# Value products on all 128 weight columns: heads and rests side by side in local and global attention

## The chip, the cores and the metric

The kernel runs on one core of one Trainium2 chip. The metric is the device time of one execution in microseconds (us), the median of several runs. The engines named are PE (TensorE; PEld is its weight load), DVE (VectorE), ACT (ScalarE), POOL (GpSimd) and SP (SyncE, whose queue issues the transfers here).

## The reference

Attention with local and global tokens, followed by a two-layer product with a squared ReLU:

```python
batch, n_heads, seq_l, seq_g, head_dim = (8, 8, 512, 32, 64)
window, scale = 32, 1 / sqrt(64)
# global queries see all 544 keys
out_g = sm(scale * q_g @ k_all.T) @ v_all
# local queries see the 32 global keys and the local ones at a distance of at most 32
s_ll = where(abs(pos[:, None] - pos[None, :]) <= window, scale * q_l @ k_l.T, -1e9)
out_l = sm(concat([scale * q_l @ k_g.T, s_ll])) @ concat([v_g, v_l])
x = concat([out_g, out_l]) as 8 * 544 rows of 8 * 64 = 512
h = maximum(x @ w_in, 0)          # w_in 512 x 2048
out = (h * h) @ w_out             # w_out 2048 x 512
```

All is float32. `sm` is a softmax over the last axis.

## The kernel before

**Two-part numbers.** Most products run in the type float32r, which holds fewer bits than float32. A value a is therefore split into a head a_h (the rounded copy, made on ACT) and a rest a_l = a - a_h (a subtraction on DVE), and a product a b is summed as a_h b_h + a_l b_h + a_h b_l. Only the first 16 heads ("plain") use plain float32.

**Steps.** A unit of attention is one head of one half sequence, 256 queries (t = 0 to 127; 16 units make one batch). One step t of the main loop interleaves: the second half of the attention of unit t - 1 (transposes of its probabilities, value product, evacuation), the first half of unit t (scores, softmax), the splitting of the inputs of unit t + 1, and one slice of the two-layer product, m = t - 9: `gemm1(m)` makes a slice h of 256 hidden columns for 256 rows (24 matmuls), `act1` and `act2` make its squared ReLU and split it into `gh` and `gl`, and `gemm2(m - 1)` adds the slice of before to the output sums (12 matmuls). The last steps have no attention.

**Order.** From t = 17 on (`FREE`) every instruction of PE, DVE and ACT keeps the order of the program text on its engine (class `InOrder`). Engines meet only in semaphores on data. So the order below is that of the queues. In step t with attention:

- `transposes(t-1)`, `scores(t)` and `gemm1(m, 0)` on PE
- `pt_split(t-1)`: ACT copies the transposed probabilities out of the PSUM tile `pt` as heads
- `softmax1(t)`: DVE adds the mask and takes the maximum of each half (`prob <- s`), and scales it
- `softmax2(t)`: ACT takes two Exp with sums
- `pt_rest(t-1)`: DVE subtracts the heads from `pt`
- jobs of the global attention (place 3), then `evac` of a finished output block
- `gemm1(m, 1)`, `av(t-1)` (the value product, into the PSUM tile `xa`), `g_scores(t)` on PE
- `softmax3(t)`: DVE makes the reciprocal, and the two halves of `prob` are scaled
- `act1(m)`: Relu on ACT, and the square on ACT or on DVE (`SQ` lists the residues of t modulo 16 with ACT)
- `x_evac(t-1)`: ACT copies the head `x_h` out of `xa`, DVE makes the rest `x_l`
- `split_head(t+1)`: ACT copies the heads `hi` of the next unit's keys, queries and values, DVE makes the rests
- `g_evac`, `g_load`, jobs (place 2), `gemm2(m-1, 0)`, `gemm2(m-1, 1)`, `act2(m)` (`gh` on ACT, `gl` on DVE), jobs (place 1)

The global attention of four heads at a time (32 queries each) is done in jobs over eight steps, twice in 16 steps: `g_soft`, `g_exp`, `g_norm`, `g_tr` (transposes into a tile of the PSUM buffer `xa`), `g_rest`, `g_split_v`, `g_av` (the value product for a pair of heads, into the same PSUM buffer `xa`, of which there is one) and `g_x`. In a period of 16, `g_av` falls in steps 1, 4, 7 and 14, `g_tr` in 3 and 13, `g_split_v` in 0, 4, 6 and 14, `g_x` in 2, 5, 8 and 15, `g_soft` in 2 and 12, `evac` in 2 and 10; `g_evac` in every odd step.

**Value product before.** For one unit: weights of 64 columns (a block of values), 128 moving columns (queries). Two blocks of keys take three products each, a middle block of 64 keys, doubled over the 128 rows, takes two, and the 32 global keys, stacked over the rows as head, head and rest, take one of 256 moving columns. That is nine matmuls into one [64, 256] result. A pair of global heads: four blocks of keys with three products and one last block, 13 matmuls of 64 weight columns and 128 moving ones.

All instructions of PE, DVE and ACT are recorded under line 52, in the helper `InOrder`; they are told apart by their tiles.

Of the kernel before, what the change touches and what calls it, by code (L numbers as in the profile page):

```python
# [7 lines left out]
F32 = mybir.dt.float32  # L8
F32R = mybir.dt.float32r
I32 = mybir.dt.int32  # L10
AF = mybir.ActivationFunctionType
# [5 lines left out]
P = 128  # L17
HALF = 256
NGR = 2 * B
NT = NGR * H  # L20
# [9 lines left out]
PLAN = [",,,b", "b,,,b", "b,,,b", "b,,b,", "b,,b,", "b,,b,", "b,,b,", "b,b,,b", "b,b,,b", "bb,bb,bb,bb", "bb,bb,bb,bb", "bbs,bb,bbs,bbs", "bbs,bbs,bbs,bbs", "bbs,bbs,bbs,bbs", "bbs,bbs,bs,s", "ss,s,s,s", "ss,s,s,s", "s,,s,", "s,,s,", "s,,s,", "s,,s,", "s,,s,", "s,,s,"]  # L30
FREE = (17, 17, 17)
LOOK = 2
SQ = (2, 3, 4, 5, 14, 15)
MUL = 9
WCH = 32

# [1 line left out]
def f(ap):  # L38
    return ap.bitcast(F32)
# [19 lines left out]
def attention_moe(  # L59
# [22 lines left out]
    def plain(t):  # L82
        return t < NPLAIN
# [41 lines left out]
    def split_head(t):  # L125

        hd = heads[t]
        raw = hd["raw"]
        if plain(t):
            return  # L130
        hi = p2.tile([P, PK], F32R, tag="hi", name=f"hi{t}")
        lo = p2.tile([P, QC + 192], F32R, tag="lo", name=f"lo{t}")
        ac.copy(hi, raw)
        ve.tensor_sub(lo, raw[:, KC : KC + QC + 192], f(hi[:, KC : KC + QC + 192]))
        ve.tensor_sub(hi[64:, :KC], raw[64:, :KC], f(hi[64:, :KC]))
        ve.tensor_sub(hi[32:64, PK - 64 :], raw[32:64, PK - 64 :], f(hi[32:64, PK - 64 :]))
        hd["hi"], hd["lo"] = hi, lo

    def scores(t):
# [45 lines left out]
    def softmax3(t):  # L185
        st = heads[t]["st"]
        pr = prob[t % 2]
        ve.tensor_scalar(out=st[:, 6:8], in0=st[:, 4:6], scalar1=1e-9, scalar2=None, op0=ALU.add)
        ve.reciprocal(out=st[:, 0:2], in_=st[:, 6:8])
        for u in range(2):  # L190
            w_ = pr[:, WIN * u : WIN * (u + 1)]
            if MUL <= t < NPLAIN:
                ac.activation(out=w_, in_=w_, func=AF.Copy, scale=st[:, u : u + 1])
            else:
                ve.tensor_scalar(out=w_, in0=w_, scalar1=st[:, u : u + 1], scalar2=None, op0=ALU.mult)
# [6 lines left out]
    def pt_split(t):  # L202
        hd = heads[t]
        if plain(t):
            pts = p2.tile([P, 512], F32, tag="gh", name=f"pts{t}")
            ac.copy(pts, pt)
            hd["pts"] = pts
            return
        ph = p1.tile([P, 640], F32R, tag="ph", name=f"ph{t}")
        pl = p1.tile([P, 256], F32R, tag="pl", name=f"pl{t}")  # L210
        ac.copy(ph[:, :256], pt[:, :256])
        ac.copy(ph[:64, 256:384], pt[:64, 320:448])
        for r in (0, 32):
            ac.copy(ph[r : r + 32, 384:640], pt[64:96, 256:512])
        hd["ph"], hd["pl"] = ph, pl

    def pt_rest(t):
        if plain(t):
            return
        ph, pl = heads[t]["ph"], heads[t]["pl"]  # L220
        ve.tensor_sub(pl, pt[:, :256], f(ph[:, :256]))
        ve.tensor_sub(ph[64:, 256:384], pt[:64, 320:448], f(ph[:64, 256:384]))

        ve.tensor_sub(ph[64:, 384:640], pt[64:, 256:512], f(ph[:64, 384:640]))

    def av(t):
        hd = heads[t]
        c = QC + KC
        if plain(t):

            xa = ps_a.tile([P, HALF], F32, tag="xa", name=f"xa{t}")
            v, pts = hd["raw"][:, c:], hd["pts"]
            mm = [
                (xa, v[:, 0:128], pts[:, 256:512]),
                (xa[:, 0:128], v[:, 64:192], pts[:, 0:128]),
                (xa[:, 128:256], v[:, 128:256], pts[:, 128:256]),
            ]
        else:
            xa = ps_a.tile([64, HALF], F32, tag="xa", name=f"xa{t}")
            vh, vl, ph, pl = hd["hi"][:, c:], hd["lo"][:, QC:], hd["ph"], hd["pl"]  # L240
            mm = []
            for u in range(2):
                o, vs, ps = xa[:, 128 * u : 128 * u + 128], slice(64 * u, 64 * u + 64), slice(128 * u, 128 * u + 128)
                mm += [(o, vh[:, vs], ph[:, ps]), (o, vl[:, vs], ph[:, ps]), (o, vh[:, vs], pl[:, ps])]
            o = xa[:, 64:192]
            mm += [(o, vh[:, 128:192], ph[:, 256:384]), (o, vl[:, 128:192], ph[:, 256:384])]
            mm.append((xa, vh[:, 192:256], ph[:, 384:640]))
        for i, (o, a, b) in enumerate(mm):
            pe.matmul(o, a, b, start=i == 0, stop=i == len(mm) - 1, skip_group_check=True)
        hd["xa"] = xa[:64, :]  # L250

    def x_evac(t):
        g, h = divmod(t, 8)
        xa = heads[t]["xa"]
        r = slice((h % 2) * 64, (h % 2) * 64 + 64)
        if g == 0:
            ac.copy(xg[r, h // 2, :], xa)
        else:
            ac.copy(x_h[r, g % 2, h // 2, :], xa)
            ve.tensor_sub(x_l[r, g % 2, h // 2, :], xa, f(x_h[r, g % 2, h // 2, :]))  # L260
        heads[t] = None

    state = {}
# [1 line left out]
    def g_load(t):  # L265

        b, grp = t // 16, (t // 4) % 2

        def cols(z, j):
            return bass.AP(z.tensor, z.offset + 64 * j, [list(z.ap[0]), [256, 2], [160, 2], [1, 32]])  # L270

        src = qg[b, grp].rearrange("p (a b) n -> p a b n", a=2)
        if plain(t):
            qz = p1.tile([P, 512], F32, tag=("ph", "gvl", "gvh", "ph")[t // 4], name=f"qz{t}")
            nc.gpsimd.memset(qz, 0.0)
            qr = p1.tile([P, 2, 2, 32], F32, tag="qr", name=f"qr{t}")
            (nc.sync if t else nc.scalar).dma_start(qr, src)
            nc.gpsimd.tensor_copy(cols(qz, 0), qr)
        else:
            qz = qgz  # L280
            qr = p1.tile([P, 2, 2, 32], F32, tag="qr", name=f"qr{t}")
            nc.sync.dma_start(qr, src)
            ac.copy(cols(qgz, 0), qr)
            ve.tensor_sub(cols(qgz, 1), qr, f(cols(qgz, 0)))
        state["qz"] = qz
# [32 lines left out]
    def g_split_v(t, pair):  # L318

        gv = state["gv"]  # L320
        gvh = p1.tile([P, 5, P], F32R, tag="gvh", name=f"gvh{t}_{pair}")
        gvl = p1.tile([P, 4, P], F32R, tag="gvl", name=f"gvl{t}_{pair}")
        ac.copy(gvh, gv)
        ve.tensor_sub(gvl, gv[:, :4, :], f(gvh[:, :4, :]))
        ve.tensor_sub(gvh[32:64, 4, :], gv[32:64, 4, :], f(gvh[32:64, 4, :]))
        state["gvs"] = gvh, gvl

    def g_soft(t):
        s = sg[:, (t // 4) % 2, :]
# [17 lines left out]
    def g_tr(t):  # L347

        s = sg[:, (t // 4) % 2, :]
        gt = ps_a.tile([P, 512], F32, tag="xa", name=f"gt{t}")  # L350
        for c in range(4):
            pe.transpose(gt[:, 128 * c : 128 * c + 128], s[:, 128 * c : 128 * c + 128], ident)
        pth = p1.tile([P, 640], F32R, tag="pth", name=f"pth{t}")
        ac.copy(pth[:, :512], gt)
        state["gpt"] = pth, gt

    def g_tr_last(t):

# [4 lines left out]
        state["ge"] = ge  # L363

    def g_rest(t):
        (pth, gt), ge = state["gpt"], state["ge"]
        ptl = p1.tile([P, 512], F32R, tag="ptl", name=f"ptl{t}")
        ac.copy(pth[:64, 512:], ge[:64, :])
        ve.tensor_sub(ptl, gt, f(pth[:, :512]))
        ve.tensor_sub(pth[64:, 512:], ge[64:, :], f(pth[:64, 512:]))  # L370
        state["gpt"] = pth, ptl

    def g_av(t, pair):
        (gvh, gvl), (pth, ptl) = state["gvs"], state["gpt"]
        xo = ps_a.tile([64, P], F32, tag="xa", name=f"gxo{t}_{pair}")
        mm = []
        for c in range(4):
            cols = slice(128 * c + 64 * pair, 128 * c + 64 * pair + 64)
            mm += [(pth[:, cols], gvh[:, c, :]), (pth[:, cols], gvl[:, c, :]), (ptl[:, cols], gvh[:, c, :])]
        mm.append((pth[:, 512 + 64 * pair : 576 + 64 * pair], gvh[:, 4, :]))  # L380
        for i, (x, y) in enumerate(mm):
            pe.matmul(xo, x, y, start=i == 0, stop=i == len(mm) - 1)
        xs = p1.tile([64, P], F32, tag="xs", name=f"gxs{t}_{pair}")
        ac.activation(out=xs, in_=xo, func=AF.Copy, scale=state["gst", t][:64, pair : pair + 1])
        state["xs"] = xs

    def g_x(t, pair):
# [71 lines left out]
    def act1(m):  # L459
        hp = moe["hp"]  # L460
        pool, tag = (p2, "gl") if m < 8 else (p1, "r")
        r = pool.tile([P, 2, HALF], F32, tag=tag, name=f"r{m}")
        ac.activation(out=r, in_=hp, func=AF.Relu)
        if m < 8 or m + LAG < NT + 8 and (m + LAG) % 16 in SQ:
            ac.activation(out=r, in_=r, func=AF.Square)
        else:
            ve.tensor_mul(r, hp, r)
        moe["r"] = r
# [33 lines left out]

    def evac(blk, tiles=(0, 1)):
        for i in tiles:
            pool, tag = ((p1, "ot"), (p2, "gl"))[i]
            ot = pool.tile([P, DM], F32, tag=tag, name=f"ot{blk}_{i}")
            ac.copy(ot, moe["o"][i])
            if blk < NGR:
# [262 lines left out]
```

## Time and profile before

| | |
|---|---|
| median of 3 runs | 1068.76 us (1068.66 to 1069.08) |
| profiled execution | 1068.82 us, span 1067.0 us |
| granted PE clock | 1.000 of full speed |
| PE busy | 1050.4 us, 98% |
| PE weight loads | 941.7 us, 88% |
| DVE busy | 856.3 us, 80% |
| ACT busy | 753.1 us, 71% |
| 16 steps in the steady part | 122.28 us |

How rows are read. A row of the timeline has the start in us from the span's start, the duration, the engine, the line, the operation, the tiles (out <- in), their shapes and how many instructions are merged (x2), and in brackets the idle time before it with what ended it. A row of groups has the busy time in us and the mean of one in ns, then the idle time before the group. A row of windows has the stretch, its length, the busy time of PE, PEld, DVE, ACT and POOL with instruction counts, the granted clock, the share of the transfer engines and GB/s. A row of waits has who waited for whom, the total, the number of times and the longest.

### The profile page before, as it was taken

What the parts mean: (1) busy time and instruction counts of PE and PEld (TensorE: products, weight loads), DVE (VectorE), ACT (ScalarE), POOL (GpSimd) and SP (SyncE); (2) the same over time, 40 slices, a digit from 0 to 9 for tenths busy, and PEclk for the clock granted to TensorE, in tenths of its full rate; (3) what the DMA queues carried; (4) which work ended last, traced back from release to release, by engine and by line L of the source; (5) the groups of instructions that cost most, each with busy time, mean ns of one, the idle gap of its engine ahead of it and who ended that gap; (6) DMA issues with size and microseconds to landing.
All of it is one profiled execution on the core that took longest, in us unless ns stands there. A gap on an engine that the chain in (4) does not pass through costs nothing.

```text
span 1067.0 us, 21142 instructions
## 1 busy us (share of the span) xinstructions
PE 1050.4 (98%) x7568; PEld 941.7 (88%) x7568; DVE 856.3 (80%) x2687; ACT 753.1 (71%) x1901; POOL 3.9 (0%) x14
## 2 busy tenths in 40 slices
PE   7999999999999999999999999999999999999998
PEld 6776889999998989998999989999999989999896
DVE  5698988898888989988888888888888888874321
ACT  5898877778777776778777777777777787774322
POOL 1000000000000000000000000000000000000000
PEclk9999999999999999999999999999999999999999
DMA  9772132223222322222322222223221322201000
GB/s 372 310 263 74 57 106 76 71 80 98 68 89 64 103 65 83 74 91 77 94 71 82 86 72 76 90 66 100 78 89 55 94 86 66 88 29 33 13 20 20
DMA packets 54312, 96.78 MB, mean 91 GB/s; under 512 B 4288, under 2 KB 29376, under 8 KB 54208
## 3 DMA queue, kind: packets, MB, share of 16 engines
q1 hardware_dynamic: 54064, 95.37, 27.2%
q8 instruction: 60, 0.98, 0.4%
q14 instruction: 44, 0.36, 0.1%
q10 hardware_dynamic: 144, 0.07, 0.0%
HBM read 86.51 MB, written 8.91 MB: 89 GB/s over the span
## 4 chain that ended last, share of the span: by engine, by line
PE 87%; ACT 7%; DVE 4%; issue 1%; DMA 0%; ACTq 0%
PE o L52 33%; PE h L52 32%; PE xa L52 7%; PE s L52 6%; PE pt L52 5%; PE gxo L52 2%; PE gs L52 2%; ACT prob L52 1%; DVE prob L52 1%; ACT r L52 1%; ACT ph L52 1%; ACT hi L52 1%; ACT ot L52 1%; PE gt L52 1%; ACT sg L52 0%
## 5 line engine op out<-in xcount | busy, mean ns | idle before, releaser
L52 PE MATMUL h<-x_h,ws 128*128 128x256 f32 x2048 | 388.9, 283 | 0.0
L52 PEld LDWEIGHTS h<-x_h,ws 128*128 128x128 f32 x2048 | 327.0, 191 | 0.5
L52 PE MATMUL o<-ws,gh 128*128 128x512 f32 x1024 | 321.3, 395 | 0.0
L52 PE MATMUL h<-x_l,ws 128*128 128x256 f32 x1024 | 289.1, 282 | 0.1
L52 PEld LDWEIGHTS o<-ws,gh 128*128 128x128 f32 x1024 | 185.5, 188 | 34.6
L52 PE MATMUL o<-ws,gl 128*128 128x512 f32 x512 | 202.6, 396 | 0.0
L52 PEld LDWEIGHTS h<-x_l,ws 128*128 128x128 f32 x1024 | 195.9, 191 | 0.9 <-DVE x_l L52 0.4
L52 ACT CAST ph<-pt 128x256 fp32r<-128x256 f32 x448 | 141.1, 341 | 67.7 <-PE pt L52 60.8
L52 ACT ACTIVATE prob<-prob,st 128x224 f32<-128x224 f32 x270 | 127.8, 475 | 61.2 <-DVE st L52 59.1
L52 ACT ACTIVATE r<-h 128x512 f32<-128x512 f32 x136 | 81.4, 599 | 112.3 <-PE h L52 112.3
L52 PEld LDWEIGHTS o<-ws,gl 128*128 128x128 f32 x512 | 96.2, 188 | 22.7
L52 DVE CUSTOM_DVE_ANT_0 prob<-s,con 128x224 f32<-128x224 f32 x256 | 90.0, 386 | 24.5 <-PE s L52 23.2
L52 DVE TENSOR_TENSOR gl<-r,gh 128x512 fp32r<-128x512 f32 x128 | 87.9, 686 | 23.3 <-ACT gh L52 20.5
L52 ACT CAST hi<-raw 128x864 fp32r<-128x864 f32 x112 | 102.5, 915 | 1.4
L52 DVE TENSOR_TENSOR r<-h,r 128x512 f32<-128x512 f32 x82 | 56.7, 692 | 51.9 <-ACT r L52 50.6
L52 PE MATMUL xa<-ph,hi 128*64 128x128 f32 x448 | 87.3, 238 | 1.6 <-DVE ph L52 1.2
L52 DVE TENSOR_TENSOR hi<-raw,hi 64x352 fp32r<-64x352 f32 x224 | 82.5, 368 | 6.4
L52 ACT CAST gh<-r 128x512 fp32r<-128x512 f32 x128 | 79.1, 618 | 9.1 <-DVE r L52 8.7
L52 DVE TENSOR_TENSOR ph<-pt,ph 64x128 fp32r<-64x128 f32 x224 | 79.6, 355 | 7.0
L52 DVE TENSOR_TENSOR lo<-raw,hi 128x448 fp32r<-128x448 f32 x112 | 69.6, 622 | 15.3 <-ACT hi L52 12.5
L52 PE MATMUL pt<-con,prob 128*128 128x128 f32 (+1 forms) x512 | 78.2, 274 | 0.7 <-ACT prob L52 0.5
L52 DVE TENSOR_SCALAR prob<-prob,st 128x224 f32<-128x224 f32 x242 | 70.7, 334 | 4.1
(80 smaller groups left out, 1572.7 us busy)
## 6 DMA issues: line engine op xcount, KB each, us to landing
raw<-in_pk_dram SPq DMA_DIRECT2D x127, 432.0 KB, 3.2
wr<-in_w_dram SPq DMA_DIRECT2D x32, 512.0 KB, 7.9
gv<-in_vg_dram SPq DMA_DIRECT2D x32, 320.0 KB, 3.3
out_dram<-ot SPq DMA_DIRECT2D x32, 256.0 KB, 2.2
qr<-in_qg_dram SPq DMA_DIRECT2D x31, 64.0 KB, 2.8
out_dram<-ot SPq DMA_DIRECT2D x8, 64.0 KB, 1.7
con<-in_consts_dram SPq DMA_DIRECT2D x2, 224.0 KB, 5.1
raw<-in_pk_dram SPq DMA_DIRECT2D x1, 304.0 KB, 3.2
```

The lines of the kernel that those rows point to most:

```text
L52: r = method(*args, **kwargs)
```

## The change

The weights of a value product become 128 columns wide: a block of values stands as 64 columns of heads with 64 columns of rests beside it. The probabilities' heads and rests stand side by side too, as 256 moving columns. One matmul then makes all four products of the parts (also rest by rest): in the rows 0 to 63 of its result stand the products with the values' heads, in the rows 64 to 127 those with the values' rests, and in two column groups those with the probabilities' heads and rests.

- `split_head`: `hi` holds keys and queries, four value blocks of head and rest (64 + 64 columns each), and the queries' rests `lo`. ACT makes two copies instead of one; DVE makes the rests of the values in an operation of its own.
- `pt_split`, `pt_rest`: one tile `ps` in place of `ph` and `pl`; the two 32-row copies of the global keys become one of 64 rows.
- `av`: four matmuls, one of 128 and three of 256 moving columns, into a whole PSUM bank. The first two write columns in two runs.
- `x_evac`: the parts are added on DVE: `xr` = heads' product - `x_h`, then + the second column group, then + the rows 64 to 127.
- `g_split_v`, `g_tr`, `g_rest`: the same parts, laid side by side in one tile.
- `g_av`: five matmuls, four of 256 moving columns and one of 64 weight columns and 128 moving ones; then a copy on ACT, two adds on DVE, and the scaling on ACT.
- `softmax3`: for units from 16 on the second half is scaled on ACT, not DVE.
- `act1`: for all steps with attention the square is made on ACT; `SQ` goes.
- `evac`: the output tile `ot` of the first half shares the buffer of `pth`; a tile of the start takes the buffer `r`; the host packs the global values twice, not three times.

```diff
-SQ = (2, 3, 4, 5, 14, 15)
...
-        hi = p2.tile([P, PK], F32R, tag="hi", name=f"hi{t}")
-        lo = p2.tile([P, QC + 192], F32R, tag="lo", name=f"lo{t}")
-        ac.copy(hi, raw)
-        ve.tensor_sub(lo, raw[:, KC : KC + QC + 192], f(hi[:, KC : KC + QC + 192]))
+        c = QC + KC
+        hi = p2.tile([P, c + 2 * VC + QC], F32R, tag="hi", name=f"hi{t}")
+        lo = hi[:, c + 2 * VC :]
+        vr = raw[:, c:].rearrange("p (b n) -> p b n", b=4)
+        vs = hi[:, c : c + 2 * VC].rearrange("p (b n) -> p b n", b=4)
+        ac.copy(hi[:, :c], raw[:, :c])
+        ac.copy(vs[:, :, :64], vr)
+        ve.tensor_sub(lo, raw[:, KC:c], f(hi[:, KC:c]))
...
-        ve.tensor_sub(hi[32:64, PK - 64 :], raw[32:64, PK - 64 :], f(hi[32:64, PK - 64 :]))
+        ve.tensor_sub(vs[:, :, 64:], vr, f(vs[:, :, :64]))
...
-            if MUL <= t < NPLAIN:
+            if MUL <= t < NPLAIN or t >= NPLAIN and u == 1:
...
-        ph = p1.tile([P, 640], F32R, tag="ph", name=f"ph{t}")
-        pl = p1.tile([P, 256], F32R, tag="pl", name=f"pl{t}")
-        ac.copy(ph[:, :256], pt[:, :256])
-        ac.copy(ph[:64, 256:384], pt[:64, 320:448])
-        for r in (0, 32):
-            ac.copy(ph[r : r + 32, 384:640], pt[64:96, 256:512])
-        hd["ph"], hd["pl"] = ph, pl
+        ps = p1.tile([P, 896], F32R, tag="ph", name=f"ph{t}")
+        pb = ps[:, :512].rearrange("p (u h n) -> p u h n", u=2, h=2)
+        ac.copy(pb[:, :, 0, :], pt[:, :256].rearrange("p (u n) -> p u n", u=2))
+        ac.copy(ps[:64, 512:640], pt[:64, 320:448])
+        ac.copy(ps[:64, 640:], pt[64:, 256:])
+        hd["ps"], hd["pb"] = ps, pb
...
     def pt_rest(t):
...
-        ph, pl = heads[t]["ph"], heads[t]["pl"]
-        ve.tensor_sub(pl, pt[:, :256], f(ph[:, :256]))
-        ve.tensor_sub(ph[64:, 256:384], pt[:64, 320:448], f(ph[:64, 256:384]))
-        ve.tensor_sub(ph[64:, 384:640], pt[64:, 256:512], f(ph[:64, 384:640]))
+        ps, pb = heads[t]["ps"], heads[t]["pb"]
+        ve.tensor_sub(pb[:, :, 1, :], pt[:, :256].rearrange("p (u n) -> p u n", u=2), f(pb[:, :, 0, :]))
+        ve.tensor_sub(ps[64:, 512:640], pt[:64, 320:448], f(ps[:64, 512:640]))
+        ve.tensor_sub(ps[64:, 640:], pt[64:, 256:], f(ps[:64, 640:]))
...
     def av(t):
...
-            xa = ps_a.tile([64, HALF], F32, tag="xa", name=f"xa{t}")
-            vh, vl, ph, pl = hd["hi"][:, c:], hd["lo"][:, QC:], hd["ph"], hd["pl"]
-            mm = []
-            for u in range(2):
-                o, vs, ps = xa[:, 128 * u : 128 * u + 128], slice(64 * u, 64 * u + 64), slice(128 * u, 128 * u + 128)
-                mm += [(o, vh[:, vs], ph[:, ps]), (o, vl[:, vs], ph[:, ps]), (o, vh[:, vs], pl[:, ps])]
-            o = xa[:, 64:192]
-            mm += [(o, vh[:, 128:192], ph[:, 256:384]), (o, vl[:, 128:192], ph[:, 256:384])]
-            mm.append((xa, vh[:, 192:256], ph[:, 384:640]))
+            xa = ps_a.tile([P, 512], F32, tag="xa", name=f"xa{t}")
+            xb = xa.rearrange("p (u h n) -> p u h n", u=2, h=2)
+            ps, vs = hd["ps"], [hd["hi"][:, c + 128 * i : c + 128 * i + 128] for i in range(4)]
+            both = bass.AP(xa.tensor, xa.offset + 64, [list(xa.ap[0]), [192, 2], [1, 64]])
+            mm = [(both, vs[2], ps[:, 512:640]), (xb[:, :, 0, :], vs[3], ps[:, 640:])]
+            mm += [(xa[:, 256 * u : 256 * u + 256], vs[u], ps[:, 256 * u : 256 * u + 256]) for u in range(2)]
...
-        hd["xa"] = xa[:64, :]
+        hd["xa"] = xa
...
     def x_evac(t):
...
-            ac.copy(xg[r, h // 2, :], xa)
+            ac.copy(xg[r, h // 2, :], xa[:64, :])
+            heads[t] = None
+            return
+        x0, x1 = x_h[r, g % 2, h // 2, :], x_l[r, g % 2, h // 2, :]
+        if plain(t):
+            ac.copy(x0, xa[:64, :])
+            ve.tensor_sub(x1, xa[:64, :], f(x0))
...
-            ac.copy(x_h[r, g % 2, h // 2, :], xa)
-            ve.tensor_sub(x_l[r, g % 2, h // 2, :], xa, f(x_h[r, g % 2, h // 2, :]))
+            xb = xa.rearrange("p (u h n) -> p u h n", u=2, h=2)
+            x0, x1 = [x.rearrange("p (u n) -> p u n", u=2) for x in (x0, x1)]
+            xr = p1.tile([P, 2, P], F32, tag="xr", name=f"xr{t}")[r]
+            ac.copy(x0, xb[:64, :, 0, :])
+            ve.tensor_sub(xr, xb[:64, :, 0, :], f(x0))
+            ve.tensor_add(xr, xb[:64, :, 1, :], xr)
+            ve.tensor_add(x1, xb[64:, :, 0, :], xr)
...
-            qz = p1.tile([P, 512], F32, tag=("ph", "gvl", "gvh", "ph")[t // 4], name=f"qz{t}")
+            qz = p1.tile([P, 512], F32, tag=("ph", "r", "gvh", "ph")[t // 4], name=f"qz{t}")
...
     def g_split_v(t, pair):
...
-        gvh = p1.tile([P, 5, P], F32R, tag="gvh", name=f"gvh{t}_{pair}")
-        gvl = p1.tile([P, 4, P], F32R, tag="gvl", name=f"gvl{t}_{pair}")
+        gvs = p1.tile([P, 9, P], F32R, tag="gvh", name=f"gvh{t}_{pair}")
+        gvh, gvl = gvs[:, :5, :], gvs[:, 5:, :]
...
-        state["gvs"] = gvh, gvl
+        state["gvs"] = gvs
...
-        pth = p1.tile([P, 640], F32R, tag="pth", name=f"pth{t}")
-        ac.copy(pth[:, :512], gt)
-        state["gpt"] = pth, gt
+        pts = p1.tile([P, 1152], F32R, tag="pth", name=f"pth{t}")
+        pc = pts[:, :1024].rearrange("p (c h n) -> p c h n", c=8, h=2)
+        gc = gt.rearrange("p (c n) -> p c n", c=8)
+        ac.copy(pc[:, :, 0, :], gc)
+        state["gpt"] = pts, pc, gc
...
     def g_rest(t):
-        (pth, gt), ge = state["gpt"], state["ge"]
-        ptl = p1.tile([P, 512], F32R, tag="ptl", name=f"ptl{t}")
-        ac.copy(pth[:64, 512:], ge[:64, :])
-        ve.tensor_sub(ptl, gt, f(pth[:, :512]))
-        ve.tensor_sub(pth[64:, 512:], ge[64:, :], f(pth[:64, 512:]))
-        state["gpt"] = pth, ptl
+        (pts, pc, gc), ge = state["gpt"], state["ge"]
+        ac.copy(pts[:64, 1024:], ge[:64, :])
+        ve.tensor_sub(pc[:, :, 1, :], gc, f(pc[:, :, 0, :]))
+        ve.tensor_sub(pts[64:, 1024:], ge[64:, :], f(pts[:64, 1024:]))
...
     def g_av(t, pair):
-        (gvh, gvl), (pth, ptl) = state["gvs"], state["gpt"]
-        xo = ps_a.tile([64, P], F32, tag="xa", name=f"gxo{t}_{pair}")
+        gvs, pts = state["gvs"], state["gpt"][0]
+        xo = ps_a.tile([P, 2, P], F32, tag="xa", name=f"gxo{t}_{pair}")
...
-            cols = slice(128 * c + 64 * pair, 128 * c + 64 * pair + 64)
-            mm += [(pth[:, cols], gvh[:, c, :]), (pth[:, cols], gvl[:, c, :]), (ptl[:, cols], gvh[:, c, :])]
-        mm.append((pth[:, 512 + 64 * pair : 576 + 64 * pair], gvh[:, 4, :]))
-        for i, (x, y) in enumerate(mm):
-            pe.matmul(xo, x, y, start=i == 0, stop=i == len(mm) - 1)
+            o = 256 * c + 128 * pair
+            mm.append((xo, pts[:, o : o + 128], gvs[:, c : c + 6 : 5, :]))
+        mm.append((xo[:64, 0, :], pts[:, 1024 + 64 * pair : 1088 + 64 * pair], gvs[:, 4, :]))
+        for i, (o, x, y) in enumerate(mm):
+            pe.matmul(o, x, y, start=i == 0, stop=i == len(mm) - 1, skip_group_check=True)
...
-        ac.activation(out=xs, in_=xo, func=AF.Copy, scale=state["gst", t][:64, pair : pair + 1])
+        ac.copy(xs, xo[:64, 0, :])
+        ve.tensor_add(xs, xo[:64, 1, :], xs)
+        ve.tensor_add(xs, xo[64:, 0, :], xs)
+        ac.activation(out=xs, in_=xs, func=AF.Copy, scale=state["gst", t][:64, pair : pair + 1])
...
-        if m < 8 or m + LAG < NT + 8 and (m + LAG) % 16 in SQ:
+        if m + LAG < NT:
...
     def evac(blk, tiles=(0, 1)):
...
-            pool, tag = ((p1, "ot"), (p2, "gl"))[i]
+            pool, tag = ((p1, "pth"), (p2, "gl"))[i]
...
-        for dup in range(3):
-            pk[:, hf, :, 32 * dup : 32 * dup + 32, c + 192 : c + 256] = v_g
+        for dup in range(2):
+            pk[:, hf, :, 64 * dup : 64 * dup + 32, c + 192 : c + 256] = v_g
```

## The prediction

> **What bounds the kernel now.** I read the page first, for the share of each engine and the chain that ended last.
>
> ```profile
> span 1067.0 us, 21142 instructions
> PE 1050.4 (98%) x7568; PEld 941.7 (88%) x7568; DVE 856.3 (80%) x2687; ACT 753.1 (71%) x1901; POOL 3.9 (0%) x14
> PE 87%; ACT 7%; DVE 4%; issue 1%; DMA 0%; ACTq 0%
> ```
>
> TensorE looks like the bound, with DVE not far behind. The kernel repeats a pattern of 16 steps (one batch), so the next view is the table of windows over one such period in the steady part.
>
> ```profile
> 254.97:377.25 122.28, 121.91 (x929) 111.53 (x927) 106.77 (x341) 90.77 (x234) 0.00 (x0) 1.00 0.26 81
> ```
>
> A period takes 122.28 us, 7.64 a step; the columns are PE, PEld, DVE and ACT. DVE works 106.77 of it, so it idles only 15.5. All three queues are issued in program order from step 17, so a wait on one holds everything behind it. Whether DVE's 13% is really free is read from the timeline of one quiet step (step 73: no global work but the copy of its scores), first DVE, then ACT.
>
> ```profile
> 539.36 0.38 DVE L52 CUSTOM_DVE_ANT_0 prob<-s,con 128x224 f32<-128x224 f32 x1
> ...
> 541.49 0.17 DVE L52 TENSOR_SCALAR st<-st 128x2 f32<-128x2 f32 x1
> 541.70 0.17 DVE L52 RECIPROCAL st<-st 128x2 f32<-128x2 f32 x1
> 541.90 0.58 DVE L52 TENSOR_SCALAR prob<-prob,st 128x224 f32<-128x224 f32 x2
> 542.89 0.69 DVE L52 TENSOR_TENSOR r<-h,r 128x512 f32<-128x512 f32 x1 [0.41 <-ACT r L52]
> 543.50 0.41 DVE L52 TENSOR_TENSOR x_l<-xa,x_h 64x256 fp32r<-64x256 f32 x1
> 544.02 0.62 DVE L52 TENSOR_TENSOR lo<-raw,hi 128x448 fp32r<-128x448 f32 x1
> 544.67 0.77 DVE L52 TENSOR_TENSOR hi<-raw,hi 64x352 fp32r<-64x352 f32 x2
> 545.47 0.48 DVE L52 TENSOR_TENSOR sg<-gs,sg 64x160 f32<-64x160 f32 x2
> 545.88 0.67 DVE L52 TENSOR_TENSOR gl<-r,gh 128x512 fp32r<-128x512 f32 x1
> 546.61 0.39 DVE L52 CUSTOM_DVE_ANT_0 prob<-s,con 128x224 f32<-128x224 f32 x1
> ```
>
> ```profile
> 540.30 0.48 ACT L52 ACTIVATE prob<-prob,st 128x224 f32<-128x224 f32 x1
> 540.69 0.19 ACT L52 ACTIVATION_READ_ACCUMULATOR prob<-prob,st 128x1 f32 x1
> ...
> 542.26 0.60 ACT L52 ACTIVATE r<-h 128x512 f32<-128x512 f32 x1 [0.92 <-PE h L52]
> 542.80 0.37 ACT L52 CAST x_h<-xa 64x256 fp32r<-64x256 f32 x1
> 543.07 0.91 ACT L52 CAST hi<-raw 128x864 fp32r<-128x864 f32 x1
> ```
>
> From one masked maximum (prob<-s) to the next is a DVE loop of 546.61 - 539.36 = 7.25 us with idle time of 0.41 and about 0.1. DVE is thus within half a microsecond of being the bound, though its share says 80%. ACT has more room: it waited 0.92 us for the first product's PSUM tile before its Relu.
>
> **The change part by part.**
>
> *TensorE.* In step 74 the nine local products and the next matmul are:
>
> ```profile
> 549.29 0.22 PE L52 MATMUL xa<-ph,hi 128*64 128x128 f32 x1
> ...
> 549.77 0.28 PE L52 MATMUL xa<-ph,hi 128*64 128x256 f32 x1
> 549.89 0.29 PE L52 MATMUL gs<-hi,qgz 128*128 128x288 f32 x1
> ```
>
> Nine take 549.89 - 549.29 = 0.60 us: eight of 0.06 and the 256-column one of 0.12. Four new ones at 0.12 take 0.48. One of them moves only 128 columns, but the next weights are now 128 wide, so I price it like the others; its other end, 0.06, would make 0.42. Gain 0.12 us in each of 112 heads: 13.4 us. The global products:
>
> ```profile
> 507.43 0.22 PE L52 MATMUL gxo<-gvh,pth 128*64 128x128 f32 x1
> ...
> 508.21 0.62 PE L52 MATMUL pt<-con,prob 128*128 128x128 f32 x4
> ```
>
> Thirteen take 0.78; the new five take 4 x 0.12 + 0.06 = 0.54, a gain of 0.24 x 32 = 7.7 us. A period of TensorE work falls by 16 x 0.12 + 4 x 0.24 = 2.9 us to 119.4. Were TensorE still the bound, the kernel would gain 21 us. No matmul of this trace writes PSUM columns in separate runs, as two of the four local ones will; they could cost nothing more, or twice 0.12 each; in the forecast below TensorE has over 1.5 us of spare time a step, so either end is covered.
>
> *DVE work.* The rows for the prices, grouped by shape:
>
> ```profile
> L52 DVE TENSOR_SCALAR prob<-prob,st 128x224 f32<-128x224 f32 x242 | 70.7, 334 | 4.1
> L52 DVE TENSOR_TENSOR lo<-raw,hi 128x448 fp32r<-128x448 f32 x112 | 69.6, 622 | 15.3 <-ACT hi L52 12.5
> L52 DVE TENSOR_TENSOR pl<-pt,ph 128x256 fp32r<-128x256 f32 x112 | 47.1, 421 | 2.8 <-ACT ph L52 1.9
> L52 DVE TENSOR_TENSOR ph<-pt,ph 64x128 fp32r<-64x128 f32 x112 | 31.7, 283 | 3.5
> L52 DVE TENSOR_TENSOR hi<-raw,hi 32x64 fp32r<-32x64 f32 x112 | 24.1, 215 | 3.2
> ```
>
> Per period: x_evac has three operations of 64x256 where it had one, +2 x 0.41 x 16 = +13.1. One softmax scaling of two goes to ACT, -0.334 x 16 = -5.3. The ten steps of 16 outside SQ lose the DVE squaring, -0.69 x 10 = -6.9. In split_head a 448-wide rest (0.62) and a 32x64 one (0.215) become two 256-wide ones (0.42 each, priced by pl): 0. The four global products get two 64x128 adds each, +8 x 0.283 = +2.3. In sum +3.2 us, to 110.0. By work alone DVE would still fit under 119.4.
>
> *ACT work.* +16 scalings of 0.48, +10 squarings of 0.63, split_head in two copies instead of one (about +0.16 x 16), the global copies +1; one 32x256 copy in pt_split goes, about 0.37 x 16. Net about +11.5, to 102: it fits too.
>
> *The order, which decides.* The scaling given to ACT stands in its queue ahead of the Relu and needs DVE's reciprocal. After it come Relu, Square (now in every step), the copy x_h, and only then can DVE's three operations of x_evac start, and behind these in DVE's queue wait lo and hi, which the next head's scores need, then gl, then the next masked maximum. So a ring runs DVE, ACT, DVE once per step, and TensorE is not in it. Times of Square and of what follows it, from a step that has one:
>
> ```profile
> 618.38 0.60 ACT L52 ACTIVATE r<-h 128x512 f32<-128x512 f32 x1 [0.93 <-PE h L52]
> 619.01 0.63 ACT L52 ACTIVATE r<-r 128x512 f32<-128x512 f32 x1
> 619.55 0.35 ACT L52 CAST x_h<-xa 64x256 fp32r<-64x256 f32 x1
> ```
>
> Let c be the masked maximum's start. The reciprocal is usable at 541.90 - 539.36 = c+2.54. The scaling on ACT holds the queue 0.40 (540.30 to 540.69 for the Exp of that shape): Relu at c+2.94. That is the c+2.90 of before, so the copy itself hides in ACT's 0.92 us of waiting. Square +0.63, x_h +0.54, its end +0.37: DVE's first x_evac operation at c+4.51. DVE finished its one remaining scaling at c+2.83, so it idles 1.68 us, and nothing in its queue may fill that. Then three dependent operations at 0.44 (0.41 and a gap of 0.03, as add and reciprocal above show): c+5.83; lo 0.44, hi 0.54, the new rest of the values 0.44, the scores' adds 0.41, gl 0.73 to the next maximum: c+8.39 instead of c+7.25.
>
> Global work on DVE ahead of the reciprocal (g_soft, g_norm, g_split_v, g_x) moves the ring by its own length, since the scaling on ACT now waits for it; before, Relu did not. So the 1.68 us stands in all 16 steps: 26.9 us. Against that go the waits that this ring swallows, from the view of waits over 150 to 950 us, 6.54 periods:
>
> ```profile
> DVE lo L52 <- ACT hi L52: 11.9, 38, 0.4
> DVE x_l L52 <- ACT x_h L52: 10.4, 18, 0.7
> DVE r L52 <- ACT r L52: 9.9, 28, 0.5
> DVE prob L52 <- PE s L52: 9.8, 19, 0.8
> ```
>
> 42.0 / 6.54 = 6.4 us. A period becomes 122.28 + 3.2 + 26.9 - 6.4 = 146.0 us, +23.7. Steps 17 to 126 close such a ring: 110 / 16 x 23.7 = +163 us. Steps 17 to 22 also split weights on DVE, work that the slack of before partly covered: a few microseconds more, I take 3. The profiled execution took 1068.82 us (span 1067.0 and 1.8 around it; the median of the three runs is 1068.76): 1068.8 + 166 = 1235 us.
>
> *Edits at nothing.* The output tile ot takes the buffer of pth: evac stands in steps 2 and 10 of a period, pth is read last in steps 1 and 7 and written again in steps 3 and 13, at the end, a full step later; without that cover the transposed global scores would wait for the output's transfer. The tag of qz and the host's packing concern the start alone. No transfer is moved, and SP's and POOL's queues keep their order. The product's PSUM buffer xa, which gt and gxo reuse, is free at about c+5.8, just before TensorE comes to them at about c+6. If it comes later, the masked maximum waits too, and it is part of the upper end.
>
> **Unknown sizes.** The dependent x_evac operations: 0.41 (their duration) to 0.48 us. The split of the values in four runs of 64: 0.42, or 0.62 at worst as for lo. ACT's copies in runs: nothing to +0.1. Two of x_evac's operations could also overlap, as r and x_l do above (0.61 from start to start for 0.69). Taken together -3 to +6 us a period: 1205 to 1275.
>
> **The rivals.**
>
> *TensorE remains the bound* (the other side: faster). It decides if the ring stays under 7.5 us a step, that is if DVE's wait for x_h is hidden. For it: DVE and ACT have the work to fit, 110 and 102 of 119.4 us, and TensorE carries 87% of the chain. Against it: the ring in the quiet step, which needs no number but start times. Result 1068.8 - 21 = 1048 us.
> The Trainium skill, "Perfetto Trace Analysis", section Identifying the Most-Contended Engine, holds that the engine with the highest occupancy is the one to shorten (for TensorE judged by the share of weight loads, 88% here). By it the sum would be 1048 us, against 1235 by the ring's rows. The trace agrees with it for the kernel as it is (TensorE is fullest and its waits are short); I do not carry it over to the changed one, because shares do not show queues waiting in a ring.
>
> *The ring binds only in part.* If the Relu did not wait for the scaling (DVE reaching the reciprocal earlier than in the quiet step), or if the global jobs filled the 1.68 us instead of adding to it, a period loses about half: 134 us, +81, 1150 us. For it: jobs of DVE do stand in ten steps. Against: they stand before the reciprocal or behind x_evac, never between.
>
> *It is slower still.* With 0.62 for the values' rest and ACT late behind its extra work in steps with evac, g_exp or gvh, half a microsecond a step more: 1290 us.
>
> **How the numbers follow.** Likeliest case 0.74, with its own range 1205 to 1275; half the ring 0.14; TensorE the bound 0.05; slower still 0.07. From 1175 to 1280 lie the likeliest case, the upper part of the half ring and the lower part of the last. A change under 0.2% (2.1 us) cannot be told from none here; it would need two opposite effects to cancel, 0.02. Faster 0.05, slower 0.93.
>
> **What would show it.** In the changed profile: DVE waits for x_h about 1.7 us in nearly every step, near 180 us in all, and TensorE waits for hi before the scores; masked maxima 8.0 to 8.4 us apart in quiet steps and a period near 146; DVE busy about 880 and ACT about 830 us; TensorE's share well under 98%; four local products in about 0.48 us. The prediction is wrong if TensorE still follows matmul on matmul, if the x_evac operations start within 0.5 us of the scaling, or if steps without global jobs stay near 7.2.

## The result and the profile after

The changed kernel takes 1262.78 us (median of 4 runs, 1260.7 to 1262.97) against 1068.77: a ratio of 1.181, 95% interval [1.1792, 1.1829], 194 us slower. The page of the changed kernel, with the span, the shares and the chain that ended last:

```profile
span 1261.1 us, 19756 instructions
PE 1092.4 (87%) x6752; PEld 951.0 (75%) x6752; DVE 892.9 (71%) x2798; ACT 813.0 (64%) x2110; POOL 3.9 (0%) x14
DVE 45%; ACT 30%; PE 17%; issue 7%; DMA 0%; ACTq 0%; DVEq 0%
```

No engine is full any more, and the chain went from TensorE to DVE and ACT. The row of windows for one period of 16 steps (steps 80 to 95):

```profile
706.34:856.01 149.67, 127.37 (x816) 112.14 (x815) 111.25 (x355) 99.66 (x264) 0.00 (x0) 0.98 0.22 66
```

This period takes 149.67 us instead of 122.28 (the five from step 32 to step 111 take 149.7 to 151.3), while DVE's work rose only from 106.77 to 111.25 and ACT's from 90.77 to 99.66. What grew is waiting. The timeline of a quiet step (step 89, the same place in its period as the step shown for the kernel before), DVE first, then ACT:

```profile
791.89 0.39 DVE L51 CUSTOM_DVE_ANT_0 prob<-s,con 128x224 f32<-128x224 f32 x1
...
794.13 0.17 DVE L51 RECIPROCAL st<-st 128x2 f32<-128x2 f32 x1
794.33 0.34 DVE L51 TENSOR_SCALAR prob<-prob,st 128x224 f32<-128x224 f32 x1
796.44 0.42 DVE L51 TENSOR_TENSOR xr<-xa,x_h 64x256 f32<-64x256 f32 x1 [1.78 <-ACT x_h L51]
796.89 0.41 DVE L51 TENSOR_TENSOR xr<-xa,xr 64x256 f32<-64x256 f32 x1
797.34 0.42 DVE L51 TENSOR_TENSOR x_l<-xa,xr 64x256 fp32r<-64x256 f32 x1
797.69 1.40 DVE L51 TENSOR_TENSOR hi<-raw,hi 128x256 fp32r<-128x256 f32 x3
799.12 0.48 DVE L51 TENSOR_TENSOR sg<-gs,sg 64x160 f32<-64x160 f32 x2
799.53 0.67 DVE L51 TENSOR_TENSOR gl<-r,gh 128x512 fp32r<-128x512 f32 x1
800.13 0.38 DVE L51 CUSTOM_DVE_ANT_0 prob<-s,con 128x224 f32<-128x224 f32 x1
```

```profile
794.39 0.48 ACT L51 ACTIVATE prob<-prob,st 128x224 f32<-128x224 f32 x1 [0.50 <-DVE st L51]
794.89 0.60 ACT L51 ACTIVATE r<-h 128x512 f32<-128x512 f32 x1
795.52 0.63 ACT L51 ACTIVATE r<-r 128x512 f32<-128x512 f32 x1
796.06 0.35 ACT L51 CAST x_h<-xa 64x256 fp32r<-64x256 f32 x1
```

The ring can be read off: DVE's reciprocal at 794.13, ACT's scaling that waited for it, Relu, Square, x_h, and DVE's first xr operation at 796.44 after 1.78 us of nothing; then everything that DVE still owes the next step. From maximum to maximum it is 8.24 us where it was 7.25. TensorE has become the one that waits:

```profile
798.78 0.68 PE L51 MATMUL s<-hi 128*128 128x224 f32 x4 [0.42 <-DVE hi L51]
```

The view of waits, DVE alone, over 150 to 1100 us (950 / 149.67 = 6.35 periods):

```profile
DVE xr L51 <- ACT x_h L51: 189.4, 101, 2.9
DVE ph L51 <- ACT ph L51: 8.6, 26, 0.3
DVE gvh L51 <- ACT gvh L51: 7.7, 12, 0.6
```

The wait for x_h is 189.4 / 6.35 = 29.8 us a period, one in each step. It exceeds the whole growth of the period, 27.4 us: DVE's added work (4.5) and a smaller new wait (1.4) stand against the waits that went.

### The profile page after: what moved, and what is told of

Its sections match the earlier page's. It is cut to its first block, busy times and chain, and to the rows that moved or that the text cites. A ratio compares the mean times of both kernels' runs of the same rounds, so it can differ in the third digit from the quotient of the medians.

```text
span 1261.1 us, 19756 instructions
## 1 busy us (share of the span) xinstructions
PE 1092.4 (87%) x6752; PEld 951.0 (75%) x6752; DVE 892.9 (71%) x2798; ACT 813.0 (64%) x2110; POOL 3.9 (0%) x14
## 4 chain that ended last, share of the span: by engine, by line
DVE 45%; ACT 30%; PE 17%; issue 7%; DMA 0%; ACTq 0%; DVEq 0%
ACT r L51 11%; DVE hi L51 10%; ACT prob L51 9%; PE h L51 8%; DVE xr L51 6%; PE o L51 6%; DVE gl L51 5%; DVE ph L51 4%; DVE prob L51 4%; DVE st L51 4%; ACT x_h L51 3%; ACT ph L51 3%; DVE sg L51 2%; DVE gvh L51 2%; DVE xg L51 2%
## 5 line engine op out<-in xcount | busy, mean ns | idle before, releaser
L51 ACT ACTIVATE prob<-prob,st 128x224 f32<-128x224 f32 x382 | 181.9, 478 | 277.3 <-DVE st L51 276.9
L51 DVE TENSOR_TENSOR xr<-xa,x_h 64x256 f32<-64x256 f32 x112 | 46.7, 417 | 207.8 <-ACT x_h L51 207.7
L51 PE MATMUL s<-hi 128*128 128x224 f32 x448 | 82.4, 310 | 88.1 <-DVE hi L51 65.2
L51 DVE TENSOR_TENSOR hi<-raw,hi 128x256 fp32r<-128x256 f32 x336 | 152.9, 455 | 6.0
L51 PEld LDWEIGHTS s<-hi 128*128 128x128 f32 x448 | 64.2, 207 | 103.4 <-ACT gh L51 73.5
L51 DVE TENSOR_TENSOR ph<-pt,ph 128x256 fp32r<-128x256 f32 x336 | 126.7, 377 | 14.3 <-ACT ph L51 9.3
L51 ACT CAST hi<-raw 128x608 fp32r<-128x608 f32 x224 | 112.6, 550 | 1.4
L51 ACT CAST ph<-pt 128x256 fp32r<-128x256 f32 x336 | 99.5, 330 | 5.8 <-PE pt L51 2.0
L51 PE MATMUL xa<-ph,hi 128*128 128x128 f32 x448 | 84.8, 292 | 19.5 <-DVE ph L51 17.9
L51 PEld LDWEIGHTS xa<-ph,hi 128*128 128x128 f32 x448 | 64.5, 189 | 31.5 <-issue 15.0
```

The lines of the kernel that those rows point to most:

```text
L51: r = method(*args, **kwargs)
```

## Experiments

All are compared with the kernel before on the same chip, where its median was 1068.65 to 1068.97 us. The changed kernel stands at 1262.8 us.

**The scaling back on DVE** (e1).

```diff
-            if MUL <= t < NPLAIN or t >= NPLAIN and u == 1:
+            if MUL <= t < NPLAIN:
```

> The changed kernel with one move undone: both softmax scalings are on DVE again, so ACT's Relu no longer stands behind an operation that needs DVE's reciprocal. Ring theory: DVE gets 16 x 0.334 = 5.3 us more work a period, but the Relu can start when its matmuls are done, at about 2.35 us after the masked maximum in place of 2.94, and no longer moves with the global jobs. DVE's wait for x_h falls from 1.77 to about 0.75 us in the seven steps without such jobs and to about nothing in the others: the period falls from 149.7 by about 18 us, the time by about 120 us to 1125 to 1155. Rival, DVE's work sets the time: 5.3 more a period, about 1300. Rival, TensorE's new matmuls set the time: no change, 1263.

1138.41 us, ratio 1.0652 [1.0636, 1.0668]. More work for DVE, and 124 us less time. Its waits:

```profile
DVE xr L51 <- ACT x_h L51: 54.5, 60, 1.7
```

207.7 us over the whole run of the changed kernel became 54.5, and the period 132.4 us (about 131.7 expected). Of the 18 us a period that went, 13 lie in the nine steps in which global jobs of DVE stand ahead of the reciprocal (1.0 to 1.7 us a step from maximum to maximum), 5 in the seven other steps (0.3 to 1.0). The engines' work as the bound is refuted in both forms.

**The squares back on DVE** (e2).

```diff
+SQ = (2, 3, 4, 5, 14, 15)
...
-        if m + LAG < NT:
+        if m < 8 or m + LAG < NT + 8 and (m + LAG) % 16 in SQ:
             ac.activation(out=r, in_=r, func=AF.Square)
```

> The changed kernel with the other move undone: the squares of ten steps in 16 are on DVE again. Ring theory: x_h comes 0.63 us earlier in these steps, but the square of 0.69 now stands ahead of x_evac on DVE; the ring gets about 0.4 us shorter in ten steps, 4 us a period: 1225 to 1245. Rival, DVE's work: 6.9 us more a period, about 1310. Rival, TensorE: 1263.

1239.38 us, ratio 1.1599 [1.158, 1.1619]: 23 us less, though DVE got 6.9 us a period more to do.

**Both moves back** (e3), the edits of e1 and e2 together:

```diff
-            if MUL <= t < NPLAIN or t >= NPLAIN and u == 1:
+            if MUL <= t < NPLAIN:
...
-        if m + LAG < NT:
+        if m < 8 or m + LAG < NT + 8 and (m + LAG) % 16 in SQ:
```

> The changed kernel with both moves undone; what is left of the change are the matmuls, the splits and the adds. Ring theory: DVE does 12.2 us more a period and is without a long wait for ACT in most steps: the period falls by about 17 us, 1130 to 1165. So the two moves would cost about 115 us of the 194, the rest of the change about 80. Rival, DVE's work: about 1345. Rival, TensorE: 1263.

1142.92 us, ratio 1.0694 [1.0678, 1.071]. DVE's wait for x_h is all but gone:

```profile
DVE xr L52 <- ACT x_h L52: 3.1, 6, 0.5
```

So of the 194 us the two moves cost 120, and the rest of the change (splits and adds against TensorE's gain) 74. The Square move alone, seen from here to e1, gains 4.5 us; it costs only where x_h already closes the ring behind the scaling.

**Without the two adds** (e4).

```diff
-            ve.tensor_sub(xr, xb[:64, :, 0, :], f(x0))
-            ve.tensor_add(xr, xb[:64, :, 1, :], xr)
-            ve.tensor_add(x1, xb[64:, :, 0, :], xr)
+            ve.tensor_sub(x1, xb[:64, :, 0, :], f(x0))
```

> The changed kernel without the two adds of x_evac (the products with rests that they would add are left out). Ring theory: the three operations of 0.44 us stand in the ring one behind the other, so two of them less take 0.88 to 0.90 us off every step, 14.3 a period: 1160 to 1170. Rival, TensorE sets the time: 1263. Rival, the ring has other slack that swallows it: about half, 1215.

1181.46 us, ratio 1.1054 [1.1037, 1.107]: 81 us less, where 98 were expected. DVE's waits show the rest:

```profile
DVE x_l L51 <- ACT x_h L51: 207.4, 112, 2.3
DVE hi L51 <- ACT hi L51: 27.0, 110, 0.3
```

With the adds gone DVE reaches the rest `lo` before ACT has made the heads, and waits 0.25 us in each step, 27 us in all. That is more than the 17 us that are missing; what stands against the other 10 was not traced. The adds had covered ACT's copy.

**The local products twice** (e5).

```diff
+            mm += mm
```

> The changed kernel with its four local value products issued twice (so the sums come out doubled): 0.48 us more TensorE work in each of 112 steps. Ring theory: TensorE waits before the scores for longer than that in every step, so 1263, at most 10 more. Rival, the new matmuls or their outputs in separate runs set the time: 0.48 x 112 = 54 us more, 1317.

1261.48 us, ratio 1.1802 [1.1784, 1.182]: no slower with 448 more matmuls, 54 us at the expectation's price. TensorE's busy time rose by 38 us, from 1092.4 to 1130.6; ten stretches fewer fell under the halved clock that the last section shows, which at 1.2 us each can hide 12 us at the most. Neither the new matmuls nor their outputs in separate runs set the time.

**The two moves in the kernel before** (e6), with nine and thirteen products:

```diff
-            if MUL <= t < NPLAIN:
+            if MUL <= t < NPLAIN or t >= NPLAIN and u == 1:
...
-        if m < 8 or m + LAG < NT + 8 and (m + LAG) % 16 in SQ:
+        if m + LAG < NT:
```

> The kernel before with the two moves alone: the second half of the softmax scaling and all squares on ACT; its value products, splits and x_evac stay. DVE gets 12.2 us less work a period and ACT 14 more. Ring theory: with a wait of 1.77 us for x_h in each step, DVE's loop is 106.8 - 12.2 + 6.7 of small gaps + 16 x 1.77 + about 2 of other waits = 131.6 us a period instead of 122.3: 1125 to 1145, 6% slower though DVE, the busier of the two, got less to do. Rival, the engines' work sets the time: no change or slightly faster, 1060 to 1069.

1193.46 us, ratio 1.1167 [1.1151, 1.1184]: slower than before by 125 us with the old products, and 48 to 68 us beyond the expected range. DVE's waits:

```profile
DVE x_l L52 <- ACT x_h L52: 214.3, 114, 3.1
DVE lo L52 <- ACT hi L52: 50.5, 110, 0.5
```

The first is what the ring says. The second was left out of the expectation: with one x_evac operation in place of three, DVE comes to `lo` 0.46 us before ACT has copied the heads of all 864 columns. 50.5 us is about what was missing. In the row of windows for this kernel's period DVE works 95.67 us, against 106.77 before, and the period is 140.83:

```profile
665.27:806.10 140.83, 126.22 (x928) 112.96 (x927) 95.67 (x316) 103.64 (x260) 0.00 (x0) 0.99 0.23 70
```

Taking work off the fuller of the two engines made the kernel 12% slower.

**x_h ahead of the Square** (e7).

```diff
         ac.activation(out=r, in_=hp, func=AF.Relu)
...
+            act1s(m)      # the Square, now behind x_evac(t - 1)
```

> The changed kernel with one change of order: ACT copies x_h right behind the Relu, and the Square comes after x_evac. No engine's work changes. Ring theory: 0.63 us less in each step, 10 us a period: about 1194 (1185 to 1205). Rivals by work, DVE's or TensorE's: 1263.

1186.24 us, ratio 1.11 [1.1082, 1.1119]: 77 us less, with no work changed, only the place of one instruction in ACT's queue. DVE's wait fell by about 0.66 us in each step:

```profile
DVE xr L51 <- ACT x_h L51: 133.4, 112, 1.6
```

**The ring opened** (e8): as e7, and

```diff
+        split_head(t + 1)     # ACT: heads of keys and queries, right behind the Exp
         softmax3(t)
+        split_rest(t + 1)     # DVE: lo and hi, into the wait for x_h
         act1(m)
...
-            split_head(t + 1)
+            split_v(t + 1)    # the values, in a tile of their own
...
+                (max(d + 4, 17), 4, g_scale, 0),
```

> As the run with x_h ahead of the Square, and the ring is opened: the heads and rests of the next unit's keys and queries are split ahead of act1 (ACT right behind the Exp, DVE right behind its scaling, into what was the wait for x_h); the values' split stays behind x_evac, in a tile of its own; the global product's last scaling goes to the next step. The work is that of the changed kernel. Ring theory: x_h comes 0.66 us earlier and the 0.98 us of lo and hi move into DVE's wait: 1.64 us off each step, 26 a period, to about 123.5: 1065 to 1095. By work alone (DVE 111 us and small gaps of 7, TensorE 119): not under 1050. Rival, the new work itself is too much: above 1140, where the kernel with both moves undone stands.

1078.32 us, ratio 1.0091 [1.0075, 1.0106], and a period of 123.92 us (123.5 expected):

```profile
599.00:722.92 123.92, 119.88 (x817) 108.71 (x816) 109.75 (x356) 98.14 (x265) 0.00 (x0) 1.00 0.26 80
```

DVE's and ACT's work in it is that of the changed kernel within 1.6 us (109.75 and 98.14 against 111.25 and 99.66), and 184 us went by order, with a tile of its own for the values. So all but 10 us of the slowdown could be taken back without taking work away. That is what the order is worth, and not a division of the slowdown by cause: with the two moves undone and the old order (e3), 74 us stayed, and the kernel before was not reordered in the same way.

**Rests on POOL** (e9, e10). As e8, with the values' rests, and then also those of the global values, on POOL:

```diff
-        ve.tensor_sub(vs[:, :, 64:], vr, f(vs[:, :, :64]))
+        nc.gpsimd.tensor_sub(vs[:, :, 64:], vr, f(vs[:, :, :64]))
...
-        ve.tensor_sub(gvl, gv[:, :4, :], f(gvh[:, :4, :]))
+        nc.gpsimd.tensor_sub(gvl, gv[:, :4, :], f(gvh[:, :4, :]))
```

> The reordered kernel with the values' rests (128x256, one per step) made on POOL, which is idle, not on DVE. Ring theory, with the ring open: DVE's queue alone sets the reordered kernel's 123.9 us a period; 0.44 x 16 = 7.0 us less brings it to 117, under TensorE's 119.4, so TensorE bounds again in the quiet steps and DVE in the heavy ones: about 120, 1053 (1045 to 1062). If POOL is slow, or slows DVE where both read SBUF, the gain is smaller: up to 1078.

> As the run with the values' rests on POOL, and the rests of the global values (g_split_v, 128x512 and 32x128, four times a period) on POOL too: 4 x 1.0 us off DVE and the wait of 0.64 for ACT's copy in two of the steps, 5.2 us a period in the steps where DVE is latest. TensorE then bounds at 119.4: 1046 to 1054. If POOL's copy comes too late for the global product in the same step, TensorE waits there and it is no better than the run with the values' rests alone.

1072.07 us, ratio 1.0034 [1.0022, 1.0046], and 1068.27 us, ratio 0.9991 [0.9982, 1.0001]: about a quarter of the expected gain, and a third, and both above the expected ranges. Groups by shape in e10, POOL's and DVE's:

```profile
L152 POOL TENSOR_TENSOR hv<-raw,hv 128x256 fp32r<-128x256 f32 x112 | 82.4, 736 | 679.9 <-ACT hv L51 671.3 <-ACT sg L51 4.8 <-issue 3.9
L51 DVE TENSOR_TENSOR gl<-r,gh 128x512 fp32r<-128x512 f32 x128 | 101.8, 795 | 26.6 <-ACT gh L51 21.8 <-DMA out_dram<-ot 0.5
```

The same `gl` took 684 ns a time in e8 and 727 in e9. The 39 of 128 that ran beside a subtraction of POOL in e9 took 805 ns on the mean, the other 89 took 692. DVE's subtraction with both inputs in SBUF gets longer while POOL reads SBUF, so part of what was moved came back: in e9 about 5 us of `gl`, where 19 of the expected gain are missing. The rest was not traced in full, but TensorE's wait ahead of `gxo` stayed (19.2 us in e8, 19.1 in e9), and steps 3, 4, 13 and 14 take 8.7 to 8.9 us in both.

**Two global jobs earlier** (e11). As e10, and

```diff
-                (d + 2, 3, g_norm),
-                (d + 3, 3, g_split_v, 0),
+                (d + 1, 2, g_split_v, 0),
+                (d + 2, 2, g_norm),
```

> As the run with both rests on POOL, and two global jobs are moved: g_split_v of the first pair two steps earlier and behind x_evac, g_norm behind x_evac in its step. In the run with both rests on POOL TensorE waits in steps 3, 4, 13 and 14 alone (0.8 us ahead of gt, 0.46 in the local products, 1.2 ahead of gxo, for DVE's x_evac). Ring theory: x_evac comes 0.75 us (steps 3 and 13) and 1.2 us (4 and 14) earlier, most of TensorE's 2.3 us a half period goes: about 119.9 a period in place of 121.8, 1055 (1050 to 1062), the first version under the kernel before. If the jobs' new places hold DVE or POOL up elsewhere: 1062 to 1069.

1061.99 us, ratio 0.9939 [0.9925, 0.9953]: the fastest kernel of this study, 0.6% under the kernel before and at the upper end of what was expected. TensorE's waits for `gt` and `gxo` are gone but for one each; in step 2, which now holds `g_split_v` beside `g_x`, `g_soft` and `evac`, DVE's loop is 9.1 us, so TensorE waits at the local products instead. Of the 21 us that the new products were worked out to save on TensorE, 7 were had this way.

## Why the prediction was right, and where it was off

The forecast was 1235 us in 1175 to 1280; the measured 1262.8 lies 28 us above it, by the mechanism that was named. All of the slowdown lies where it was forecast: from the masked maximum of step 17 to that of step 127 it is 194.6 us.

- *The ring.* The first xr operation was forecast at c+4.51 after the masked maximum; it is at 796.44 - 791.89 = c+4.55 (the forecast's terms, as written, add up to c+4.48). The wait was forecast at 1.68 us in every step, and is 1.78 in this one. That it adds to the global jobs and is not filled by them holds: 101 waits in 6.35 periods are one in each of 16 steps. Undoing the scaling (e1), shifting x_h (e7) and opening the ring (e8) all moved the time as the ring says, within 9 us of the middle of the expected range. Taking out the adds (e4) fell 17 us short and the moves in the kernel before (e6) went 48 to 68 us beyond, each with a wait for ACT's copy `hi` that the expectation had left out.
- *Terms that were mis-sized.* The period was forecast at 146.0 us and is 149.7, on the mean of five 150.2. The quiet step was forecast at 8.39 us and is 8.24, so the missing time is in the other steps. The wait is 29.8 us, not 26.9: the scaling holds ACT's queue 0.50 us (794.39 to 794.89), not the 0.40 of an Exp; in step 10 the two `evac` copies stand ahead of it and make the wait 2.27 us. DVE's busy time grew by 4.5, not 3.2: the two scalings together had taken 0.58 us in the quiet step and one alone takes 0.34, so the move saves 0.24 a step, 3.8 a period, and not 5.3. The x_evac operations last 417 to 427 ns, not 410, which is 0.5 a period. And x_evac's buffer was costed at nothing: TensorE does come to `xa` before x_evac is done (waits over the whole run),

```profile
ACT gxs L51 <- DVE gxs L51: 50.6, 31, 2.3
PE gxo L51 <- DVE x_l L51: 33.5, 28, 2.6
```

  and behind it ACT waits for DVE's two adds before the last scaling, which makes the next `pt_split` late and costs DVE the 1.4 us of `ph` shown above. Together 2.9 + 1.3 + 1.4 = 5.6 is more than the 3.7 that was missing; against it stand a wait of 1.1 us a period for ACT's copy of `pth`, which went, and shorter gaps between DVE's operations. 3.7 us in 6.9 periods are 25 of the 28 us, and with the mean of five periods, 4.2 too many, 29. The 3 us set aside for the splitting of weights were about 1.6.
- *TensorE.* Four local products were priced at 0.48 us; they take 645.49 - 645.02 = 0.47 in step 73, so 128 weight columns behind 128 moving ones cost like the others, and outputs in separate runs nothing that shows in the sum of the four:

```profile
645.02 0.63 PE L51 MATMUL xa<-ph,hi 128*128 128x128 f32 x4
645.49 0.29 PE L51 MATMUL gs<-hi,qgz 128*128 128x288 f32 x1
```

  The period of TensorE's work was worked out at 119.4; the reordered kernel, where it waits little, shows 119.88 busy.
- *The rivals.* "TensorE remains the bound" fails in e5, "the engines' work" in e1, e2, e3 and e6. "The ring binds only in part" (1150 us) fails by the wait for x_h, which stands in full in all 16 steps. "Slower still" (1290 us) is as near to the measured time as the forecast is: its values' rest at 0.62 us did not come (0.42), its late ACT did in the one step named above. The rule of the Trainium skill ("Perfetto Trace Analysis", Identifying the Most-Contended Engine) that was weighed there would have given 1048 us; its shares read 98% and 80% before, and 87% and 71% after. The run e6 is the plain counterexample in this case: less work for the second fullest engine, 125 us lost.

What stays open is how the 74 us of splits and adds in e3 divide; only the adds were taken out by themselves, and in the changed kernel.

## What to carry to other kernels

Where engines work through queues in a fixed order, look for the ring that closes once per iteration and add up its start times; shares of 80% and 71% hid one with half a microsecond of slack here. Moving an operation to the emptier engine is free only if what it waits for comes earlier than what already stood in its place in that queue: one 0.5 us scaling cost 124 us here, most of it in the steps where DVE's global jobs then delayed ACT's Relu. Before work is moved, try the order: an operation that closes the ring goes ahead of one that does not (x_h before Square, 77 us), and work that the next iteration needs goes into the wait (with the later scaling a further 108 us).

## What was not expected of the hardware

TensorE's granted clock, 1.000 on average before, is 0.976 after. Windows of 3.4 us around step 73 of the changed kernel (the last three columns are the clock, the transfer engines' share and GB/s):

```profile
636.80:640.20 3.40, 1.50 (x10) 1.04 (x9) 2.44 (x6) 3.09 (x8) 0.00 (x0) 1.00 0.00 0
640.20:643.60 3.40, 3.40 (x17) 3.40 (x18) 3.04 (x12) 1.04 (x4) 0.00 (x0) 0.50 0.42 134
643.60:647.00 3.40, 3.40 (x24) 3.15 (x24) 0.56 (x2) 2.23 (x5) 0.00 (x0) 1.00 0.00 1
```

After a stretch in which TensorE was busy 1.50 of 3.40 us, the clock is halved for the next 3.4 us: 17 matmuls where 24 fit after it. The same stands around 694.7 us (1.41 us busy before it), 752.8 (1.42) and 845.0 (1.44). In step 73 the Relu then waits for its matmuls and DVE 2.81 us for x_h, and the step takes 9.26 us from maximum to maximum where the same step a period later takes 8.24. This is no rival for the slowdown. There are 17 such stretches of 3.4 us before the kernel's end; steps 79 and 95, into which those of 694.7 and 845.0 reach, take 9.86 and 9.87 us, and step 111, without one, takes 9.87. At 1.2 us each, the most that like steps show (step 25 against step 89), all would make 20 of the 194 us. The Trainium skill, "TensorE: Matmul & The Clock Gate", Part 1, has windows of 3.4 us and says that an idle one throttles, and tells of a kernel in which short idle times between groups of matmuls were enough; here windows that were 41 to 44% busy were.

POOL's subtractions lengthen DVE's: `gl` 684 ns in e8, 727 in e9, 795 in e10. The Trainium skill, "SBUF — State Buffer", says that a VectorE instruction with two SBUF inputs contends with a GpSimd instruction that reads SBUF; these runs agree (in e10 the 42 `gl` beside a subtraction of POOL take 1006 ns on the mean, the 86 others 692). The operation `x_l`, with one input from PSUM, was not touched: 110 of its 112 run beside POOL in e9 and 111 in e10, at 427 ns as in e8 without POOL.
